# Plain float32 second products for the whole first tile, doubled zeros' products in the front, and two steps of the weight conversion moved from VectorE to GpSimd

## The chip, the cores and the metric

The kernel runs on one core of one Trainium2 chip. The metric is the device time of one execution in microseconds (us), taken as the median of the runs shown. TensorE is called PE in the profile, VectorE DVE, ScalarE ACT, GpSimd POOL and SyncE SP; PEld is the loading of weights into TensorE. SP issues the DMAs.

## The reference

A gated linear attention (an mLSTM) over 4 batches, 8 heads, 768 steps and head width 40 gives `x` of 3072 rows and 320 columns; behind it stands a feed-forward layer with a smooth rectifier.

```python
for t in range(S):
    m_new = np.maximum(f_gate[:, :, t] + m, i_gate[:, :, t])
    f_stab = np.exp(f_gate[:, :, t] + m - m_new); i_stab = np.exp(i_gate[:, :, t] - m_new)
    C = f_stab * C + i_stab * einsum('bhd,bhe->bhde', vt, kt)
    n = f_stab * n + i_stab * kt
    y[:, :, t] = sigmoid(o_gate) * einsum('bhde,bhe->bhd', C, qt) / np.maximum(abs(n . qt), 1.0)
x = y.transpose(0, 2, 1, 3).reshape(3072, 320)
h = x @ w_in                                                 # 320 -> 2048
g = np.where(h >= 1, h, np.where(h <= -1, 0, (h + 1) ** 2 / 4))
out = g @ w_out                                              # 2048 -> 320
```

## The kernel before

The 768 steps are cut into 6 chunks of 128 (L), so there are 24 blocks `n` = chunk x 4 + batch. Four blocks make one tile `j` of 512 rows for the feed-forward layer, so there are 6 tiles. `w_in` is worked through in 16 slices `fc` of 128 columns. `mm1(j, fc)` is 8 matmuls of 128x512 into a PSUM tile `psh`, of which there are two, and three passes (`r`: a relu and a square on ACT, a maximum and minimum on DVE) make `g` of it. `mm2` multiplies `g` by the same slice of `w_out` (128 rows of 320 columns) into four PSUM tiles `pso`, one for each 128 rows of the tile, two steps `x` after its `mm1` (LAG = 2).

Float32 products are made in one of two ways. In the split way both operands are parted into a rounded high part and a rest (`gh`, `gl` from `r`; `oh` and `ol` from the weights) and three fp32r matmuls are made per 128 rows. In the plain way one float32 matmul is made of `r` and of the unparted weights `of`; the profile shows such a matmul as two records and its names as `pso<-ow,r`. `PLAIN_FC` says for how many slices of tile 0 the second products are plain. The weights of these slices are then parted in tile 1, at the even `fc`.

The weights come in as 64-bit words (the host passes float32 seen in another layout) and are converted on the chip by `words`: ACT makes the magnitude `mg`, one engine puts the sign into the upper 16-bit half of each word (`halves[:, :, 1]`), GpSimd the low bits into the lower half (`halves[:, :, 0]`), a maximum clamps `mg`, and a DVE instruction (`SCALAR_TENSOR_TENSOR win<-mg,win` or `ow<-mg,ow`) shifts and joins them. Pieces of `w_in` have 128x768 elements (`win`, from `wraw`), pieces of `w_out` 128x640 (`ow`). There are 8 of each; one piece of `w_in` is converted in the front, the others during tile 0 by `split_next`, which runs ahead of `fc` by `DUE`. After `words`, `split` makes the rounded part `wh` on ACT and the rest `wl` on DVE; the first products need both. `win` and `mg` have one buffer each, so a conversion waits for the one before it.

Ahead of tile 0 stands the front: the attention of the blocks 0 to 3, written out by hand as the list `STEPS`. `E` and `A` are the products that make a block's matrix of exponents in PSUM, `x` its exponentials on ACT, `s` the scores on PE, `m` their product on DVE, `h` the transposition of the gates, `v` a scaling of `v` on GpSimd, `u` the matmuls with `v`, `y`, `z` and `t` the rest of a block. `w1` means: one matmul of zeros (128x512, bf16) ahead of the next product that opens a PSUM tile; its result is overwritten. `w9` at the start makes nine.

During tile 0 the attention of the blocks 4 and on runs in slots `slot(FRONT + x)`. Its parts: `select` (GpSimd, `AFFINE_SELECT Abc`) masks the sums that a DMA from `a_d` has spread over all rows, `decay` (ACT, 8 activations `Abc<-Abc,nA`), `score`, `main` and `carry_on` (`C`). The gates of a chunk (`gate_piece`) are some 17 small DVE instructions of 32 rows, from the scan `m<-fi_t` to `ex<-m,ah`.

Within `STEPS` the program order of each engine is as written. Behind it the framework's scheduler sets the order of each engine's instructions, so an edit in one place can move the instructions of others. Every engine works through its own list strictly in that order.

Of the kernel before, what the change touches and what calls it, by code (L numbers as in the profile page):

```python
# [13 lines left out]
ALU = mybir.AluOpType  # L14
# [17 lines left out]

LAG = 2

PLAIN_FC = 4

# [13 lines left out]


STEPS = (
# [3 lines left out]
)  # L58

HALF = 64  # L60
# [4 lines left out]
TINY = 2.0  # L65
# [30 lines left out]
def mlstm_ffn_kernel(ctx, tc, qk, qn, vk, og, fi0, fi, w_in, w_out, cst, out):  # L96
    nc = Core(tc)
# [197 lines left out]
    def words(out, raw):  # L295

        n = raw.shape[1] * raw.shape[2] // 2
        hi = raw.rearrange("p k (f w) -> p (k f) w", w=2)[:, :, 1]  # L300
        quarter = raw.rearrange("p k f -> p (k f)").bitcast(U16).rearrange("p (f w) -> p f w", w=4)
        out = out.rearrange("p k f -> p (k f)").bitcast(I32)
        halves = out.bitcast(U16).rearrange("p (f w) -> p f w", w=2)
        mg = stage.tile([P, n], F32, name="mg", bufs=1)
        nc.scalar.activation(mg, hi.bitcast(F32), AF.Abs, scale=65536.0)
        nc.vector.tensor_scalar(out=halves[:, :, 1], in0=quarter[:, :, 3], scalar1=0x8000, scalar2=None,
                                op0=ALU.bitwise_and)

        nc.gpsimd.tensor_scalar(out=halves[:, :, 0], in0=quarter[:, :, 1], scalar1=1 / 8192, scalar2=-4095.5 / 8192,
                                op0=ALU.mult, op1=ALU.add)  # L310
        nc.vector.tensor_scalar_max(mg, mg, TINY)
        nc.vector.scalar_tensor_tensor(out=out, in0=mg.bitcast(I32), scalar=3, in1=out,
                                       op0=ALU.logical_shift_left, op1=ALU.bitwise_or)

# [18 lines left out]
    def convert(kind, i):  # L333
        raw = raws.pop((kind, i))
        if kind == "in":
            sl = slice(2 * i * P, 2 * (i + 1) * P)
            w = stage.tile([P, 3, 2 * P], F32, name="win", bufs=1)
            words(w, raw)
            yield
            yield from split(wh[:, :, sl], wl[:, :, sl], w)  # L340
        else:
            of[i] = ow.tile([P, 656], F32, name="ow")[:, :2 * DM].rearrange("p (k e) -> p k e", k=2)
            words(of[i], raw)
            if 2 * i >= PLAIN_FC:
                yield
                yield from split_out(i)
# [283 lines left out]
    for n in range(NS):  # L630
        j, r = divmod(n, NTC)
        s0 = FRONT + OFFS[n - B] if j else 0
# [10 lines left out]
    def slot(i):  # L643
        for n, kind in sorted(plan.get(i, ()), key=lambda x: (list(order).index(x[1]), x[0])):
            if (n, kind) not in gens:
                gens[n, kind] = order[kind](n)
            next(gens[n, kind])
            c, b = divmod(n, B)
            if kind == "main":
                at[n] = at.get(n, 0) + 1  # L650
                if b == 0 and at[n] == 1:
                    with behind(("r", "act")):
                        sigmoid(c)
                if b == B - 1 and at[n] == 1 and c + 1 < NC:
                    load_og(c + 1)
# [18 lines left out]
    def parts(r):  # L674
        gh = mo.tile([P, TT], F32R, name="gh", bufs=3)
        nc.scalar.copy(gh, r)
        gl = mo.tile([P, TT], F32R, name="gl", bufs=3)
        nc.vector.tensor_tensor(out=gl, in0=r, in1=gh.bitcast(F32), op=ALU.subtract)
        return gh, gl
# [110 lines left out]
    for x in range(NG + LAG):  # L790
        j, fc = divmod(x, NFC)
        if x < NG:
# [6 lines left out]
            if fc == 0:  # L799
                ops[j] = [ps_o.tile([P, 512], F32, name="pso") for _ in range(NTC)]  # L800
            if j == 1 and fc % 2 == 0 and fc < PLAIN_FC:
                with tc.issue_after(mark["r", "act"].ins), tc.issue_after(mark["r", "dve"].ins):
# [11 lines left out]
            with behind(("v", "pool")):  # L814
                slot(FRONT + x)
            gs[x] = parts(r) if j or fc >= PLAIN_FC else (r,)
        if x >= LAG:
# [60 lines left out]
```

## Time and profile before

| | |
|---|---|
| median of 3 runs | 534.55 us (534.29 to 538.14) |
| profiled execution: its own time, its span | 537.02 us, 535.2 us |
| PE, DVE, ACT, POOL busy | 501.2, 370.9, 297.0, 147.3 us |
| granted TensorE clock, mean | 0.945 of full speed |
| first product of tile 0 | at 36.6 us |
| first product of tile 1 | at 151.85 us |

The span is 1.8 us shorter than the profiled execution's own time. A row of the timeline gives the start in us, the duration in us, the engine, the source line, the operation, what it writes and reads and how many instructions are merged; in brackets stands the idle time before it and what ended that. A row of a window gives its length, each engine's busy time with the number of its instructions, the granted clock and the DMAs' share.

### The profile page before, as it was taken

How to read it: one execution, taken by the hardware profiler on the slowest of the kernel's cores; microseconds unless marked ns; L12 is line 12 of the kernel's file. 1: busy time of each engine (PE TensorE's matmuls, PEld its weight loads, DVE VectorE, ACT ScalarE, POOL GpSimd, SP SyncE). 2: the span in 40 equal slices, each digit the busy share in tenths (PEclk: the TensorE clock that was granted, in tenths of full speed). 3: DMA queues.
4: the chain of work that ended last, by engine and by line, in shares of the span. 5: the costliest groups of instructions: out<-in, count | busy, mean ns of one | idle time of the engine just before them, and what ended most of it. 6: DMA issues, size and time to landing. Idle time of an engine off the chain costs nothing.

```text
span 535.2 us, 9288 instructions
## 1 busy us (share of the span) xinstructions
PE 501.2 (94%) x3563; PEld 432.8 (81%) x3563; DVE 370.9 (69%) x689; ACT 297.0 (55%) x588; POOL 147.3 (28%) x148
## 2 busy tenths in 40 slices
PE   8985979998999999989999979899999999999996
PEld 5763768777879889978888858688888898989985
DVE  5579989888879767768576849777657766443342
ACT  6235777644748563467644435755468344455553
POOL 4115513333433223433052515143411212000000
PEclk9577989967999999999999979899999999999999
DMA  8837454454252213251122234032333100010001
GB/s 245 261 114 241 157 182 151 139 185 153 80 156 72 57 51 103 79 171 58 29 79 69 87 103 149 3 91 91 112 105 114 39 1 1 1 50 1 0 1 50
DMA packets 29648, 51.31 MB, mean 96 GB/s; under 512 B 10124, under 2 KB 20004, under 8 KB 29604
## 3 DMA queue, kind: packets, MB, share of 16 engines
q1 hardware_dynamic: 29604, 50.72, 30.3%
q8 instruction: 28, 0.46, 0.4%
q14 instruction: 16, 0.13, 0.1%
HBM read 46.67 MB, written 4.04 MB: 95 GB/s over the span
## 4 chain that ended last, share of the span: by engine, by line
PE 59%; DVE 8%; ACT 7%; DMA 2%; issue 1%; POOL 1%; ACTq 0%; POOLq 0%
PE psh L79 26%; PE pso L79 21%; PE psa L79 11%; ACT Abc L79 2%; ACT r L79 2%; DMA Abc<-a_d 2%; DVE r L79 1%; DVE z L79 1%; ACT L79 1%; DVE gl L79 1%; DMA out<-r 1%; DVE ow L79 1%; ACT gh L79 1%; DVE C L79 1%; POOL Abc L79 1%
## 5 line engine op out<-in xcount | busy, mean ns | idle before, releaser
L79 ACT ACTIVATE r<-psh,half 128x512 f32<-128x512 f32 x96 | 65.3, 684 | 101.9 <-PE psh L79 98.8
L79 PE MATMUL psh<-xh,wh 128*128 128x512 f32 x288 | 106.1, 426 | 13.3 <-DVE r L79 10.9
L79 PE MATMUL pso<-ow,gh 128*128 128x320 f32 x368 | 113.9, 312 | 1.0 <-DVE ow L79 1.0
L79 PE MATMUL pso<-oh,gh 128*128 128x320 f32 x368 | 112.8, 315 | 0.0
L79 DVE SCALAR_TENSOR_TENSOR r<-psh,r 128x512 f32<-128x512 f32 x96 | 65.8, 686 | 65.7 <-ACT r L79 65.3
L79 PE MATMUL pso<-oh,gl 128*128 128x320 f32 x368 | 105.2, 311 | 0.0
L79 PE MATMUL psh<-xh,wl 128*128 128x512 f32 x288 | 102.3, 411 | 0.1
L79 DVE TENSOR_TENSOR gl<-r,gh 128x512 fp32r<-128x512 f32 x92 | 67.2, 733 | 30.4 <-ACT gh L79 29.4
L79 ACT CAST gh<-r 128x512 fp32r<-128x512 f32 x92 | 56.7, 617 | 51.7 <-DVE r L79 50.8
L79 PEld LDWEIGHTS pso<-ow,gh 128*128 128x128 f32 x368 | 69.6, 189 | 4.2 <-DVE ow L79 1.2
L79 PEld LDWEIGHTS pso<-oh,gh 128*128 128x128 f32 x368 | 69.0, 189 | 4.4 <-ACT gh L79 0.2
L79 PEld LDWEIGHTS psh<-xh,wh 128*128 128x128 f32 x288 | 52.9, 200 | 24.1 <-DVE r L79 12.5
L79 PEld LDWEIGHTS psh<-xh,wl 128*128 128x128 f32 x288 | 56.4, 198 | 14.0 <-DVE wl L79 0.8
L79 PEld LDWEIGHTS pso<-oh,gl 128*128 128x128 f32 x368 | 66.7, 188 | 0.6
L79 PE MATMUL psh<-xl,wh 128*128 128x512 f32 x192 | 62.7, 408 | 0.0
L79 ACT ACTIVATE r<-r 128x512 f32<-128x512 f32 x96 | 60.2, 632 | 2.2
L79 ACT ACTIVATE Abc<-Abc,nA 128x128 f32<-128x128 f32 x160 | 49.5, 389 | 19.0 <-POOL Abc L79 18.8
L79 POOL TENSOR_TENSOR m<-m 128x1024 bf16<-128x1024 f32 x16 | 32.0, 1999 | 56.3 <-DVE m L79 45.3
L79 POOL TENSOR_TENSOR v<-vk,G 128x328 f32<-128x328 f32 x36 | 31.0, 864 | 54.4 <-issue 31.6
L79 PEld LDWEIGHTS psh<-xl,wh 128*128 128x128 f32 x192 | 37.6, 197 | 8.9
L79 POOL TENSOR_TENSOR C<-C,dec 120x369 f32<-120x369 f32 x16 | 14.6, 910 | 89.2 <-PE psa L79 89.2
L79 PE MATMUL psa<-raw 40*128 40x128 f32 x320 | 33.9, 300 | 3.5 <-ACT nA L79 1.7
(187 smaller groups left out, 709.3 us busy)
## 6 DMA issues: line engine op xcount, KB each, us to landing
Abc<-a_d SPq DMA_DIRECT2D x20, 512.0 KB
raw<-in_qk SPq DMA_DIRECT2D x48, 160.0 KB
vk<-in_vk SPq DMA_DIRECT2D x20, 324.0 KB
wraw<-in_w_in SPq DMA_DIRECT2D x8, 768.0 KB
wraw<-in_w_out SPq DMA_DIRECT2D x8, 640.0 KB
sig<-in_og SPq DMA_DIRECT2D x6, 640.0 KB
out<-r SPq DMA_DIRECT2D x24, 160.0 KB
qn<-in_qn SPq DMA_DIRECT2D x20, 180.0 KB
```

What stands on the lines that cost most here:

```text
L79: r = getattr(self.engine, name)(*args, **kwargs)
```

## The change

`PLAIN_FC` goes from 4 to 16: all second products of tile 0 are plain. The weights of `w_out` are no longer parted in tile 0, and all 8 pieces are parted in tile 1, where 2 were before; the parting of `r` into `gh` and `gl` falls away in tile 0 for 12 of 16 slices. In `STEPS` each `w1` but one becomes `w2`, and `E1 A1` with a `w1` of its own moves from ahead of `k0` to behind `m00`. In `words` the sign becomes a comparison and a multiplication on GpSimd, and the clamp of `mg` moves there too.

```diff
-PLAIN_FC = 4
+PLAIN_FC = 16
...
-    "Lg Li Lo Lq0 Lv0 Lq1 Lw0 Lf Lq2 Lv2 Lq3 Lw1 Lc o w9 E0 g0 p A0 E1 A1 k0 x00 w1 s0 h0 x01 m00 v0 x10 m01 w1 s1 "
-    "x11 v1 m10 c w1 u0 m11 w1 E2 A2 x20 w1 s2 y0 x21 v2 m20 m21 w1 u1 z0 w1 E3 A3 x30 e w1 s3 v3 y1 x31 t0 m30 m31 "
-    "w1 u2 z1 y2 w1 u3 t1 z2 y3 w1 t2 z3 t3 d g1 "
+    "Lg Li Lo Lq0 Lv0 Lq1 Lw0 Lf Lq2 Lv2 Lq3 Lw1 Lc o w9 E0 g0 p A0 k0 x00 w2 s0 x01 m00 w1 E1 A1 h0 v0 x10 m01 w2 s1 "
+    "x11 v1 m10 c w2 u0 m11 w2 E2 A2 x20 w2 s2 y0 x21 v2 m20 m21 w2 u1 z0 w2 E3 A3 x30 e w2 s3 v3 y1 x31 t0 m30 m31 "
+    "w2 u2 z1 y2 w2 u3 t1 z2 y3 w2 t2 z3 t3 d g1 "
...
-        nc.vector.tensor_scalar(out=halves[:, :, 1], in0=quarter[:, :, 3], scalar1=0x8000, scalar2=None,
-                                op0=ALU.bitwise_and)
+        nc.gpsimd.tensor_scalar(out=halves[:, :, 1], in0=quarter[:, :, 3], scalar1=32768.0, scalar2=32768.0,
+                                op0=ALU.is_ge, op1=ALU.mult)
...
-        nc.vector.tensor_scalar_max(mg, mg, TINY)
+        nc.gpsimd.tensor_scalar(out=mg, in0=mg, scalar1=TINY, scalar2=None, op0=ALU.max)
```

The order of the instructions moves with it. On PE in the front, ahead of the scores of block 0 and behind the sums of block 0 (`pick` are the sums' selecting columns, `raw` the scores, `late_t,idb` the mask that opens a block's exponents), what is added is marked with +:

```order
 L82 LDWEIGHTS pick
 L82 MATMUL psh<-ac_179,pick 128x128
+L82 LDWEIGHTS zeros
+L82 MATMUL pso<-zeros 128x512
+L82 LDWEIGHTS zeros
+L82 MATMUL pso<-zeros 128x512
+L82 MATMUL pso<-raw 128x128 x8
+L82 LDWEIGHTS zeros
+L82 MATMUL pso<-zeros 128x512
 L82 LDWEIGHTS idb
 L82 MATMUL pso<-late_t,idb 128x512
```

The scores of block 0 with two zeros' products now stand ahead of block 1's exponents, where they stood behind them with one.

On ACT in the first slices of tile 0, from the conversion's `wh` of the second piece of `w_in`, before:

```order
L79 ACTIVATE r<-psh,half 128x512
L79 ACTIVATE r<-r 128x512
L79 CAST wh<-win 128x3x256
L79 ACTIVATE mg<-wraw 128x640
L79 ACTIVATE r<-psh,half 128x512
L79 ACTIVATE r<-r 128x512
L79 ACTIVATE G<-psa 128x128
L79 ACTIVATE nA<-psa 128x32
L79 ACTIVATE Abc<-Abc,nA 128x128 x12
L79 ACTIVATE mg<-wraw 128x768
```

And there in the changed kernel (the first `r<-psh` here is that of the third slice):

```order
L79 CAST wh<-win 128x3x256
L79 ACTIVATE mg<-wraw 128x640
L79 ACTIVATE G<-psa 128x128
L79 ACTIVATE nA<-psa 128x32
L79 ACTIVATE Abc<-Abc,nA 128x128 x16
L79 ACTIVATE r<-psh,half 128x512
L79 ACTIVATE mg<-wraw 128x768
L79 ACTIVATE Abc<-Abc,nA 128x128 x4
L79 ACTIVATE r<-psh,half 128x512
L79 ACTIVATE Abc<-Abc,nA 128x128 x4
L79 ACTIVATE r<-r 128x512 x2
```

The 24 exponentials of the blocks 4 to 6 now stand ahead of the squares `r<-r` of the third and fourth slice, and these ahead of the next `wh`; before, the squares and that `wh` came first. On DVE the two `r<-psh,r` of these slices stand ahead of the gates of chunk 2 in the changed kernel, and the join of the third piece (`win<-mg,win`) behind all but two of the gates' instructions. On SP the three DMAs that spread the sums of chunk 1 (`Abc<-a_d`) stood behind the load of the third piece of `w_in` and stand ahead of it.

On POOL at the same place, from the conversion of the second piece of `w_in` on, before:

```order
L79 TENSOR_SCALAR win<-wraw 128x768
L79 TENSOR_TENSOR ow<-ow,G 128x328 x2
L79 TENSOR_SCALAR win<-wraw 128x768
L79 TENSOR_SCALAR ow<-wraw 128x640
L79 COPY ex<-fi_t 32x128
L79 TENSOR_TENSOR ow<-ow,G 128x328
L79 AFFINE_SELECT Abc<-Abc 128x1024 x3
L79 TENSOR_TENSOR v_630<-vk,G 128x328
L79 TENSOR_TENSOR v_770<-vk,G 128x328
```

And in the changed kernel, from the clamp of that piece on:

```order
L79 TENSOR_SCALAR mg<-mg 128x768
L79 TENSOR_SCALAR win<-wraw 128x768 x2
L79 COPY ex<-fi_t 32x128
L79 AFFINE_SELECT Abc<-Abc 128x1024 x2
L79 TENSOR_SCALAR mg<-mg 128x640
L79 AFFINE_SELECT Abc<-Abc 128x1024
L79 TENSOR_TENSOR v_642<-vk,G 128x328
L79 TENSOR_TENSOR v_779<-vk,G 128x328
L79 TENSOR_SCALAR win<-wraw 128x768 x2
L79 TENSOR_SCALAR ow<-wraw 128x640 x2
L79 TENSOR_TENSOR ow<-ow,G 128x328
L79 TENSOR_SCALAR mg<-mg 128x768
```

Each piece now has three passes on POOL. Those of the third piece of `w_in` (the second `win<-wraw`) stood ahead of the three selects and now stand behind them and behind both scalings of `v`.

## The prediction

> **What bounds the kernel now.** I read the page's busy times first, then windows of the span, then the timeline at the places where PE waits.
>
> ```profile
> span 535.2 us, 9288 instructions
> PE 501.2 (94%) x3563; PEld 432.8 (81%) x3563; DVE 370.9 (69%) x689; ACT 297.0 (55%) x588; POOL 147.3 (28%) x148
> ...
> 12.37:26.02 13.65, 13.65 (x73) 11.09 (x72) 7.97 (x17) 3.82 (x13) 2.49 (x3) 0.50 0.90 264
> ...
> 36.60:157.50 120.90, 106.69 (x606) 88.82 (x606) 104.97 (x184) 74.14 (x151) 47.60 (x44) 0.87 0.51 163
> ...
> 36.60:59.25 22.65, 16.70 (x56) 12.19 (x56) 22.38 (x44) 10.86 (x19) 12.16 (x10) 0.78 0.84 281
> 59.25:157.50 98.25, 89.99 (x554) 76.63 (x552) 82.60 (x141) 63.28 (x133) 35.43 (x34) 0.90 0.43 136
> 157.50:300.00 142.50, 139.52 (x1096) 123.54 (x1093) 106.11 (x198) 84.09 (x171) 47.45 (x43) 1.00 0.27 81
> ```
>
> In a window's row stand its length, the busy time of PE, PEld, DVE, ACT and POOL, and the granted clock. PE is the bound over the whole, but not everywhere. From 157.5 to 300 us it works at full clock and idles 2% (139.52 of 142.50). In tile 0, from 36.6 to 157.5 us (157.5 is where the products of block 8 with `v` end, with 18 first and 16 second products done), it is DVE that is full: 104.97 of 120.90 us, in the first 22.65 us even 22.38. PE idles there 14.2 us and has a clock of 0.87. In the front, from 12.37 to 26.02 us, PE is busy without a gap and yet at half clock. The change touches these two places; what lies behind 157.5 us it touches only through the parting of weights in tile 1.
>
> **The change part by part. Plain second products cost PE time.** A plain slice and a split slice, each up to what follows it, at full clock:
>
> ```profile
> 65.84 2.32 PE L79 MATMUL pso<-ow,r 128*128 128x320 f32 x8
> 67.99 0.27 PE L79 MATMUL psa<-ident,ex 128*128 128x128 f32 x1
> ...
> 463.31 0.31 PE L79 MATMUL pso<-oh,gh 128*128 128x320 f32 x1
> ...
> 465.04 0.63 PE L79 MATMUL psh<-xh,wh 128*128 128x512 f32 x2
> ```
>
> The plain slice takes 67.99 - 65.84 = 2.15 us, the split one 465.04 - 463.31 = 1.73. Twelve slices more are plain: 12 x 0.42 = 5.0 us of PE.
>
> **What leaves DVE in tile 0**, by groups of 36.6 to 157.5 us:
>
> ```profile
> L79 DVE TENSOR_TENSOR gl<-r,gh 128x512 fp32r<-128x512 f32 x12 | 8.8, 742 | 1.1 <-ACT gh L79 1.1
> ...
> L79 DVE TENSOR_TENSOR ow<-ow,oh 128x640 fp32r<-128x640 f32 x7 | 7.0, 1006 | 0.0
> ...
> L79 DVE TENSOR_SCALAR win<-wraw 128x768 uint16<-128x768 uint16 x7 | 6.1, 875 | 0.1
> L79 DVE TENSOR_SCALAR ow<-wraw 128x640 uint16<-128x640 uint16 x8 | 4.8, 602 | 0.7 <-DMA wraw<-in_w_out 0.6
> L79 DVE TENSOR_SCALAR mg<-mg 128x768 f32<-128x768 f32 x7 | 4.7, 677 | 0.0
> L79 DVE TENSOR_SCALAR mg<-mg 128x640 f32<-128x640 f32 x8 | 4.6, 578 | 0.0
> ```
>
> The 12 `gl` go (8.8), six of the seven `ol` move to tile 1 (6 x 1.0 = 6.0), and the sign and the clamp go to POOL (6.1 + 4.8 + 4.7 + 4.6 = 20.2). DVE keeps 105 - 35 = 70 us. That ends DVE as the bound of tile 0.
>
> **What comes to POOL.** The sign is of the kind that POOL does already for the low bits; the clamp, one float32 input on POOL at this size, is not in the trace.
>
> ```profile
> L79 POOL TENSOR_SCALAR win<-wraw 128x768 uint16<-128x768 uint16 x7 | 10.4, 1482 | 24.5 <-DVE wl L79 13.3 <-issue 7.9 <-DVE ac L82 2.0
> ...
> L79 POOL TENSOR_SCALAR_AFFINE_SELECT Abc<-Abc 128x1024 f32<-128x1024 f32 x7 | 8.8, 1257 | 8.2 <-DMA Abc<-a_d 8.2
> L79 POOL TENSOR_SCALAR ow<-wraw 128x640 uint16<-128x640 uint16 x7 | 7.2, 1027 | 10.0 <-DMA wraw<-in_w_out 7.1 <-PE psh L79 2.8
> ```
>
> Signs: 7 x 1.48 + 8 x 1.03 = 18.6 us. For the clamp the bounds are the select's time by elements (1257 x 768/1024 = 0.94 us and 0.79) and that of the low bits (1.48 and 1.03); I take the lower, the select being float32 too: 7 x 0.94 + 8 x 0.79 = 12.9, at most 18.6. POOL goes from 47.6 to 79 us, at most 85, of some 115: it fits, but it is no longer idle, and everything queued behind a pass waits.
>
> **Term 1, the front.** How zeros' products and the narrow products go at half and full clock:
>
> ```profile
> 19.95 3.48 PE L82 MATMUL psa<-ow,Abc 128*128 128x41 f32 x16
> ...
> 23.23 0.88 PE L82 MATMUL psa<-ident,y 128*128 128x128 f32 x3
> 23.90 0.63 PE L82 MATMUL psh<-zeros 128*128 128x512 bf16 x1
> 24.32 1.06 PE L82 MATMUL psh<-late_t,idb 128*128 128x512 bf16 x2
> ...
> 26.03 0.38 PE L82 MATMUL pso<-zeros 128*128 128x512 bf16 x1
> ...
> 27.66 1.87 PE L82 MATMUL pso<-ow,Abc 128*128 128x41 f32 x16
> 29.37 0.52 PE L82 MATMUL pso<-ident,y 128*128 128x128 f32 x3
> ```
>
> The same 16 narrow matmuls take 3.28 us at half clock (19.95 to 23.23) and 1.71 at full. A zeros' product takes 0.42 us at half (23.90 to 24.32), so 0.21 at full; the exponents of a block take 1.71 (24.32 to 26.03), so 0.86. What brings the clock up at 26.02 is a window that ends with wide, full-height products (zeros, `late_t`, `pick`); what stood ahead, narrow products of 41 columns or of 40 rows, kept PE busy and did not. In the changed program the window ahead of the drop at 12.37 us holds block 1's exponents (0.86 us, from before that window) and three more zeros' products (0.63) of 3.41 us; I expect that the clock then stays up. Halving the 13.65 us gives 6.8; the change has 12 zeros' products more, 12 x 0.21 = 2.5: **-4 us**. If the clock doesn't stay up, four of them lie in the half-clock stretch and eight outside: 4 x 0.42 + 8 x 0.21 = +3.4. PE sets the end of the front, since ACT and DVE have 3.82 and 7.97 of those 13.65 us. The moved `E1 A1` costs at most its 0.86 us ahead of `h0`, hidden behind the exponentials on ACT; without that cover it is lost.
>
> **Term 2, from tile 0's first product to that of slice 4** (36.6 to 59.25 us). Here the order speaks against the change.
>
> ```profile
> 2.83 0.48 DVE L82 TENSOR_TENSOR_SCAN m<-fi,m 96x128 f32<-96x128 f32 x1 [1.90 <-DMA fi<-in_fi]
> ...
> 6.43 0.14 DVE L82 COPY carry<-m 32x1 f32<-32x1 f32 x1
> ...
> 47.95 1.22 PE L79 MATMUL psh<-xh,wh 128*128 128x512 f32 x2 [5.95 <-DVE r L79]
> ...
> 52.53 2.37 POOL L79 TENSOR_SCALAR_AFFINE_SELECT Abc<-Abc 128x1024 f32<-128x1024 f32 x2 [1.18 <-DMA Abc<-a_d]
> ...
> 59.66 3.31 ACT L79 ACTIVATE Abc<-Abc,nA 128x128 f32<-128x128 f32 x11
> ...
> L79 ACT ACTIVATE r<-psh,half 128x512 f32<-128x512 f32 x18 | 12.0, 678 | 9.6 <-PE psh L79 9.5
> L79 ACT ACTIVATE r<-r 128x512 f32<-128x512 f32 x18 | 11.1, 629 | 0.3
> ...
> L79 ACT CAST wh<-win 128x768 fp32r<-128x768 f32 x7 | 5.8, 825 | 12.6 <-DVE win L79 12.6
> ...
> L79 DVE SCALAR_TENSOR_TENSOR r<-psh,r 128x512 f32<-128x512 f32 x16 | 10.8, 681 | 3.6 <-ACT r L79 3.4
> ...
> L79 DVE SCALAR_TENSOR_TENSOR ow<-mg,ow 128x640 int32<-128x640 int32 x8 | 7.5, 933 | 0.0
> ...
> L79 DVE SCALAR_TENSOR_TENSOR win<-mg,win 128x768 int32<-128x768 int32 x7 | 6.6, 948 | 0.2
> ```
>
> Slice 2 waited 5.95 us, to 47.95. DVE loses the passes ahead of it, but POOL now does three passes where it did one; I leave that start as it is (a gain of 2 us and a loss of 2 are both possible). Then ACT has 24 exponentials ahead of the squares of slices 2 and 3. They can begin when the selects have the spread sums: 52.5 before, some 2 us earlier now, since SP issues these DMAs ahead of a weight load; with a select of 1.2, at about 51.5. ACT: 24 x 0.30 + 2 x 0.68 + 2 x 0.63 = 9.8, to 61.3. DVE must then finish `r` of both and all of chunk 2's gates, since the join stands behind them: the same recurrences of chunk 0 took 3.7 us (2.83 to 6.57), two `r` and the join take 2 x 0.68 + 0.95 = 2.3, and `wh` on ACT is 0.83: 68.1 for slice 4 instead of 59.25, **+9**. In that time two carries and more are done that came later before (1.3 us): **+8**. Bounds: +3, if ACT starts on the second exponentials late anyway and DVE's gates fall into the gap; +11, if the DMAs land as before.
>
> **Term 3, from slice 4 to the mark at 157.5.** Before: 98.25 us, PE busy 89.99, clock 0.90. A clock of 0.90 is a fifth of the time at half; half of that is lost, 0.10 x 98.25 = 9.8. So PE's work at full clock is 80.2 us, and with the plain products 85.2, less the 1.3 done already, 83.9. With DVE relieved (about 58% where it was 84%), I take the idle share of the stretch behind 157.5 us, 2%, so 1.8, and one half-clock window after the wait of term 2, 1.7: 87.4, **-11**. Bounds: -14 (no idle at all), and 0 (below, the shared port).
>
> **Term 4, tile 1.** Six more partings of weights, 6 x 1.0 us on DVE and as many casts on ACT, lie beside PE in a stretch where DVE has 106 of 142.5 us. I take **+1**; if that cover were gone, 6.
>
> Sum: -4 + 8 - 11 + 1 = -6 us against the profiled execution's span of 535.2, which lies 1.8 us under its own time of 537.02 and is within 0.1% of the median of 534.55. I set the -6 against the median: **528.5 us**.
>
> **The rivals.**
>
> *The clock stays low in the front.* For it: PE was busy in all of 12.37 to 26.02 us and the clock was 0.50 all the same, so busy time alone does not lift it. Against it: the lift at 26.02 came with wide products. Price: +3.4 instead of -4, so 535.9. The Trainium skill, in "TensorE: Matmul & The Clock Gate", section "What's actually happening", says that one busy window of some 3.4 us releases the clock and an idle one throttles it; by PE's busy time that is contradicted by this stretch, and by it zeros' products could not help where PE never idles.
>
> *POOL and DVE share a port, and POOL becomes the bound (the slower side).*
>
> ```profile
> 38.45 2.22 POOL L79 TENSOR_SCALAR win<-wraw 128x768 uint16<-128x768 uint16 x1 [7.87 <-issue]
> ...
> 39.65 1.24 DVE L82 TENSOR_TENSOR_SCAN m<-fi_t,m 32x128 f32<-32x128 f32 x1
> ```
>
> A scan that takes 0.48 us alone (2.83) took 1.24 beside a POOL pass, and that pass 2.22 where the mean is 1.48: each waited for the other. If POOL's passes and DVE's conversion steps go one after the other, a pair of slices needs 2 x 1.48 + 0.94 and 2 x 1.03 + 0.79 on POOL, two joins and `wl` on DVE (0.95 + 0.93, and 0.95 for `wl`, which I take like the join), ACT's 0.83, and POOL's attention, (47.6 - 10.4 - 7.2) / 8 = 3.8: 14.2 us. From slice 4 there are 7 pairs to the mark: 99 us. Above 12.5 us for a pair (87.4 / 7) POOL decides; at 14.2 term 3 is +1 instead of -11, and the sum is +6: 540.5. Against it: POOL's own sum is at most 85 of 115 us. The Trainium skill, in "SBUF — State Buffer", section "SBUF: two separate sides", calls the port pair of DVE and GpSimd an exclusive lock that is held for a whole instruction. The two rows above agree; by this rule moving passes from DVE to GpSimd relieves the port of nothing.
>
> *The early wait of term 2 does not come, and the rest does.* ACT gets its sums early and slice 4 starts as before: -4 + 0 - 13 + 1 = -16, so 518.5.
>
> *DVE was full but not the limit*, since PE waited for chains of attention that remain: term 3 is -3, the sum +2 with the front's gain: 536.5.
>
> **How the numbers follow.** My forecast, 524 to 533, has 0.45; the missing early wait (517 to 523) 0.13; the low clock 0.18; DVE not the limit 0.12; the shared port 0.12. The predicted time is that of the forecast. A measurement tells about 1% (5.3 us, so 529.2 and 539.9) from no change. Of the forecast about 0.30 lies below 529.2, with the 0.13 that is 0.43 for faster; for slower I count 0.10 of the port and 0.07 of the two cases near 536, 0.17; 0.40 remain. The range goes from 518 to 540.5: it leaves out a little at each end, no more than 2 in 10.
>
> **What would show it.** The clock in 12.37 to 26.02 us at 1.00 and tile 0's first product near 32.6 us (term 1); PE idle for 6 to 9 us ahead of slice 4, behind a DVE join or `wh` (term 2); PE at 95% or more behind that, DVE under 65% (term 3); no gap above 0.5 us in tile 1 (term 4). POOL passes of `win` above 1.6 us in the mean, or PE waiting for DVE joins that wait for POOL's clamps throughout tile 0, would make it wrong on the slow side; an early start of slice 4 on the fast side.

## The result and the profile after

The changed kernel takes 550.99 us in the median of 4 runs (549.08 to 551.92), the kernel before 534.42 in the 4 beside them (530.65 to 538.14). The ratio is **1.0292, 95% interval 1.0230 to 1.0353**: slower by 2.9%, where 528.5 us was forecast and the range ended at 540.5. The ratios here leave out disturbed runs; the medians are over all runs.

The page of the changed kernel: busy times, and the chain that ended last by engine (that of before has POOL with 1%).

```profile
span 548.9 us, 9190 instructions
PE 504.5 (92%) x3527; PEld 427.5 (78%) x3527; DVE 352.2 (64%) x645; ACT 291.7 (53%) x576; POOL 232.5 (42%) x180
...
PE 64%; POOL 17%; DVE 7%; issue 5%; ACT 4%; DMA 2%; ACTq 0%; POOLq 0%; DVEq 0%
```

DVE is relieved (370.9 to 352.2 us) and POOL has gone from 147.3 to 232.5, 85 us more over the whole span, where the forecast gave it 31 to 37 more in tile 0. And POOL is on the chain.

Windows by the prediction's terms, before (first four rows) and after (the others): from tile 0's first product to that of slice 4, from there to that of slice 18, from there to that of tile 2, and the rest. The columns are as before.

```profile
36.61:59.25 22.64, 16.69 (x56) 12.18 (x56) 22.36 (x44) 10.85 (x19) 12.16 (x10) 0.78 0.84 281
59.25:159.26 100.01, 91.16 (x569) 77.60 (x567) 84.24 (x146) 65.02 (x134) 36.17 (x35) 0.90 0.43 138
159.26:231.06 71.80, 70.85 (x558) 63.19 (x558) 56.15 (x104) 42.54 (x90) 23.83 (x23) 1.00 0.27 82
231.06:535.20 304.14, 289.85 (x2184) 256.36 (x2184) 187.22 (x340) 162.63 (x305) 67.12 (x60) 0.98 0.19 60
...
36.69:69.81 33.12, 20.50 (x68) 15.50 (x69) 22.67 (x46) 18.76 (x48) 29.10 (x19) 0.71 0.46 156
69.81:174.47 104.66, 93.43 (x449) 72.09 (x449) 60.23 (x93) 49.14 (x88) 92.16 (x53) 0.85 0.39 132
174.47:248.79 74.32, 73.35 (x617) 65.14 (x615) 60.65 (x111) 45.26 (x94) 25.65 (x24) 1.00 0.29 88
248.79:548.90 300.11, 288.25 (x2184) 255.16 (x2184) 188.87 (x340) 162.59 (x305) 67.75 (x60) 0.99 0.20 60
```

| stretch | before | after | difference | forecast |
|---|---|---|---|---|
| front | 36.61 | 36.69 | +0.1 | -4 |
| first product to slice 4 | 22.64 | 33.12 | +10.5 | +8 |
| slice 4 to slice 18 | 100.01 | 104.66 | +4.7 | -11 |
| rest of tile 1 | 71.80 | 74.32 | +2.5 | +1 |
| behind tile 1 | 304.14 | 300.11 | -4.0 | 0 |
| span | 535.2 | 548.9 | +13.7 | -6 |

(The last row but one is PE's idle time, 14.3 against 11.9 us, and the clock; the change touches nothing there.) These are windows of one execution each. The kernel before, profiled once more below, had 21.75 us in the second row and 104.97 in the third. So the 10.5 us ahead of slice 4 are clear of what two executions of one kernel differ by, and the 4.7 behind it are not.

In tile 0 POOL is busy 29.10 + 92.16 = 121.3 us of 137.8, DVE in the second stretch 60.23 of 104.66: the bound went from DVE to POOL. POOL's work alone is nearly as long as both stretches together were before (122.65). The chain that ended last shows it too; between slice 4 and slice 18 its shares by line are (the view ends the row there):

```profile
by line: POOL win L79 18.9%; POOL mg L79 17.6%; issue 16.4%; POOL ow L79 13.9%; PE psh L79 10.8%; PE pso L79 8.1%; POOL v L79 4.7%; POOL Abc L79 3.3%; POOL C L79 3.1%; DVE win L79 2.3%; PE psa L79 1.0%; DVE xl L79 0.3%; DVE xh L79 0.3%; POO
```

The passes of the conversion on POOL are half of it (18.9 + 17.6 + 13.9%). POOL's groups from 36.69 to 174.47 us, busy time and mean of one:

```profile
L79 POOL TENSOR_SCALAR win<-wraw 128x768 uint16<-128x768 uint16 x14 | 31.9, 2278 | 1.0
L79 POOL TENSOR_SCALAR ow<-wraw 128x640 uint16<-128x640 uint16 x14 | 25.5, 1819 | 1.0
L79 POOL TENSOR_SCALAR mg<-mg 128x640 f32<-128x640 f32 x8 | 17.2, 2150 | 6.8 <-ACT mg L79 6.7
L79 POOL TENSOR_SCALAR mg<-mg 128x768 f32<-128x768 f32 x7 | 15.8, 2252 | 3.3 <-ACT mg L79 2.9
```

Signs and low bits together take 57.4 us, where the forecast had 18.6 + 10.4 + 7.2 = 36.2; the clamps take 33.0, where it had 12.9. A pair of slices costs POOL 2 x 2.28 + 2.25 + 2 x 1.82 + 2.15 = 12.6 us of conversion, and with the forecast's 3.8 of attention 16.4.

The front: its window, POOL's first conversion (shortest, median and longest of a sign and a low-bit pass), then who waits for its clamp:

```profile
12.37:26.02 13.65, 10.26 (x80) 7.72 (x79) 6.64 (x15) 3.83 (x14) 8.70 (x6) 0.87 0.88 265
...
L82 POOL TENSOR_SCALAR win<-wraw x2: 1062/2062/3062, 12.7 to 15.8; 128x768 uint16<-128x768 uint16 x2
...
16.96 2.14 POOL L82 TENSOR_SCALAR mg<-mg 128x768 f32<-128x768 f32 x1
19.13 1.48 DVE L82 SCALAR_TENSOR_TENSOR win<-mg,win 128x768 int32<-128x768 int32 x1 [6.24 <-POOL mg L82]
...
21.27 1.09 PE L82 MATMUL psa<-ow,Abc 128*128 128x41 f32 x8 [2.83 <-DVE Abc L82]
```

DVE stood idle for 6.24 us here, and yet the sign took 3.06 us and the clamp 2.14: they are long by themselves, not through DVE. The join waits for the clamp, the product `m` (`Abc<-psh,Abc`) stands behind the join on DVE, and PE waits for that, 2.83 us.

### The profile page after: what moved, and what is told of

The parts are those of the page before. It is cut to its first block, busy times and chain, and to the rows that moved or that the text cites. A ratio compares the mean times of both kernels' runs of the same rounds, so it can differ in the third digit from the quotient of the medians.

```text
span 548.9 us, 9190 instructions
## 1 busy us (share of the span) xinstructions
PE 504.5 (92%) x3527; PEld 427.5 (78%) x3527; DVE 352.2 (64%) x645; ACT 291.7 (53%) x576; POOL 232.5 (42%) x180
## 4 chain that ended last, share of the span: by engine, by line
PE 64%; POOL 17%; DVE 7%; issue 5%; ACT 4%; DMA 2%; ACTq 0%; POOLq 0%; DVEq 0%
PE psh L79 28%; PE pso L79 25%; PE psa L79 10%; POOL win L79 4%; POOL mg L79 4%; POOL ow L79 4%; DMA Abc<-a_d 2%; POOL v L79 1%; POOL Abc L79 1%; ACT r L79 1%; ACT Abc L79 1%; POOL win L82 1%; DVE gl L79 1%; DVE z L79 1%; POOL C L79 1%
## 5 line engine op out<-in xcount | busy, mean ns | idle before, releaser
L79 PE MATMUL pso<-oh,gh 128*128 128x320 f32 x320 | 99.3, 313 | 0.0
L79 PE MATMUL pso<-ow,gh 128*128 128x320 f32 x320 | 98.4, 310 | 0.0
L79 PE MATMUL pso<-oh,gl 128*128 128x320 f32 x320 | 92.7, 312 | 0.0
L79 DVE TENSOR_TENSOR gl<-r,gh 128x512 fp32r<-128x512 f32 x80 | 62.3, 779 | 29.4 <-ACT gh L79 28.1
L79 ACT CAST gh<-r 128x512 fp32r<-128x512 f32 x80 | 49.5, 619 | 51.8 <-DVE r L79 49.5
L79 PEld LDWEIGHTS psh<-xh,wh 128*128 128x128 f32 x288 | 55.2, 207 | 18.1 <-ACT wh L79 4.3
L79 PEld LDWEIGHTS pso<-oh,gh 128*128 128x128 f32 x320 | 60.1, 188 | 3.5
L79 PEld LDWEIGHTS pso<-ow,gh 128*128 128x128 f32 x320 | 60.2, 188 | 2.8
L79 PEld LDWEIGHTS pso<-oh,gl 128*128 128x128 f32 x320 | 58.2, 188 | 0.8
L79 ACT ACTIVATE Abc<-Abc,nA 128x128 f32<-128x128 f32 x160 | 49.3, 389 | 17.8 <-POOL Abc L79 17.6
L79 POOL TENSOR_SCALAR mg<-mg 128x640 f32<-128x640 f32 (+1 forms) x15 | 33.0, 2198 | 10.0 <-ACT mg L79 9.6
```

Source lines behind the costliest of these rows:

```text
L79: r = getattr(self.engine, name)(*args, **kwargs)
```

## The experiments

"Price theory": a sign or a clamp costs POOL far more than I charged, and POOL's sum is the limit of tile 0. Against it stand the port theory (the passes are long because DVE holds a shared port), the wait theory (the loss is the scheduler's order ahead of slice 4) and the chain theory (the round of magnitude, clamp and join through one buffer). First the parts of the change, apart. Rows are windows from slice 4 to slice 18 unless said otherwise.

**Both conversion steps back on DVE**

```diff
-        nc.gpsimd.tensor_scalar(out=halves[:, :, 1], ... op0=ALU.is_ge, op1=ALU.mult)
+        nc.vector.tensor_scalar(out=halves[:, :, 1], ... op0=ALU.bitwise_and)
-        nc.gpsimd.tensor_scalar(out=mg, in0=mg, scalar1=TINY, scalar2=None, op0=ALU.max)
+        nc.vector.tensor_scalar_max(mg, mg, TINY)
```

> The changed kernel with the sign and the clamp back on DVE; the plain second products and the front's new list stay. Price theory (the two moved passes cost POOL far more than the 1.48 and 0.94 us charged: 3.06 and 2.14 us in the front of the changed kernel, where DVE stood idle, and POOL is then the limit of tile 0): the loss goes, slice 4 starts at 59 to 62 us, POOL is under 50 us in tile 0, the median is 525 to 532 us. Wait theory (the loss comes from the order, ACT's 24 exponentials ahead of the squares before slice 4, whoever converts): slice 4 still starts behind 66 us and the median is 536 to 543. In the front the join of the first piece no longer waits for POOL's clamp, so the gap of 2.83 us at 18.44 goes and the first product of tile 0 comes at 32.5 to 34 us instead of 36.7.

Measured: 533.14 us, ratio 0.9948 (0.9891 to 1.0005), one us above the price theory's range. First product to slice 4, then slice 4 to slice 18, in a profiled execution of 537.54 us, 4 us above the median:

```profile
32.04:54.55 22.51, 16.56 (x55) 12.22 (x56) 22.27 (x40) 10.72 (x19) 11.65 (x11) 0.73 0.78 281
54.55:158.32 103.77, 94.94 (x520) 73.63 (x518) 73.72 (x132) 55.04 (x116) 35.50 (x35) 0.90 0.42 133
```

The loss is gone, and the wait ahead of slice 4 with it (22.51 us). But on ACT the squares of slices 2 and 3 stand ahead of the exponentials again in this kernel, so that it doesn't part the wait theory from the price theory; the last experiment does. The front reaches tile 0 at 32.04 us. The second stretch, 103.77 us, is no shorter than before (100.01 and 104.97 in two profiles); the next experiment but one bears on that.

**The conversion alone** (the kernel before, with the two lines of the change)

> The kernel before with only the sign and the clamp on POOL. Price theory: POOL needs about 3.1 + 1.06 + 2.2 + 2.6 + 0.92 + 2.2 = 12.1 us for a pair of slices plus some 3.8 of attention, 16 us where the pair took 12 to 14 before: 14 to 20 us slower, 548 to 555. Wait theory: the order of ACT decides; if the 24 exponentials do not stand ahead of the squares here, the time is within 4 us of before. DVE theory (DVE's full list was the limit of tile 0 and relief from 20 us of passes pays): 522 to 530.

Measured: 561.34 us, ratio 1.0493 (1.0408 to 1.0578), even above the expected 548 to 555. From slice 4:

```profile
73.34:182.20 108.86, 92.16 (x498) 77.33 (x498) 71.97 (x110) 58.38 (x104) 90.36 (x53) 0.84 0.38 127
```

POOL has 90 us here as in the changed kernel. The conversion is the whole loss; without the other parts it is larger. Tile 0's first product came at 40.57 us, 4 us later than in the changed kernel.

**The plain products alone** (`PLAIN_FC = 16` in the kernel before)

> The kernel before with only PLAIN_FC = 16. It costs PE 12 x 0.42 = 5.0 us and takes 8.8 (the rests of r) and 6.0 us (six partings) from DVE in tile 0, which was full there: if DVE is the limit of tile 0, the gain is 8 to 10 us on DVE less nothing on PE, 525 to 529; if chains of attention are the limit and DVE only full, it is the 5 us of PE, 537 to 540. I expect 530.

Measured: 536.57 us, ratio 1.0031 (0.9973 to 1.0088). From slice 4, and the front:

```profile
54.95:159.25 104.30, 94.88 (x520) 73.50 (x518) 76.66 (x131) 55.30 (x116) 35.87 (x35) 0.90 0.42 134
...
12.37:26.02 13.65, 13.45 (x115) 10.83 (x114) 9.06 (x20) 7.45 (x24) 3.15 (x3) 0.87 0.89 258
```

In the stretch from slice 4 the kernel before, profiled once more, had:

```profile
58.48:163.45 104.97, 94.19 (x568) 80.05 (x566) 87.56 (x151) 65.21 (x134) 36.95 (x36) 0.87 0.43 134
```

DVE falls from 84.24 and 87.56 us to 76.66, and the stretch lies between the two of the kernel before. PE idles 9.4 us, where it idled 8.9 and 10.8: the relief of DVE did not take away its waits. My own figure of 530 was missed. The interval leaves -1.4 to +4.7 us, and 5.0 is what the plain products were to cost PE, so what the relief bought in time is not resolved.

**The front's list alone**

> The kernel before with only the new list of the front. If the clock stays up from 12.37 us as it did in the changed kernel (at 1.00 up to 22.4 us), the first product of tile 0 comes 3 to 4 us earlier, at about 33 us, and the median is 529 to 532. If tile 0 is bound by the conversion on DVE from the start, not by the first product, half of it is lost there: 532 to 535. Low clock: 537 to 538.

Measured: 533.63 us, ratio 0.9979 (0.9935 to 1.0023). The front's stretch:

```profile
12.37:26.02 13.65, 13.28 (x122) 10.68 (x124) 10.18 (x22) 7.52 (x24) 2.79 (x4) 1.00 0.90 266
```

The clock stays at 1.00, and the first product comes at 31.13 us. In the time it isn't resolved: the interval reaches over 1.

**The kernel before once more**, for its front

> The kernel before once more, for a second look at its front. If the half clock from 12.37 to 26.02 us belongs to the old list of the front, it shows again and the first product of tile 0 comes at 36.6 us. If it belongs to where the clock's windows of 3.41 us happen to lie in that execution, the front is shorter or the half-clock stretch lies elsewhere, as in the kernel with only the plain products, which has the old list and reached tile 0 at 32.64 us.

```profile
12.37:26.02 13.65, 13.65 (x77) 10.94 (x77) 8.29 (x17) 3.97 (x14) 3.14 (x3) 0.56 0.90 259
```

The half clock lasts as long here as in the first profile, with PE busy in all of it; it only begins 1.5 us later:

```profile
13.88:27.53 13.65, 13.65 (x75) 10.57 (x76) 7.09 (x16) 4.14 (x14) 2.69 (x3) 0.50 0.88 258
```

In the three profiles of the old list with the conversion on DVE the clock from 12.37 to 26.02 us was 0.50, 0.56 and (plain products alone) 0.87, and the first product came at 36.61, 36.73 and 32.64 us. So two of three executions of the old list have the long stretch at half clock and one has not; the profile that I took the term from was one of the two, and none of the three had 1.00. With the new list and the clamp on DVE the clock was 1.00 there and tile 0 began at 31.13 to 32.81 us in all four profiles that computed the sign.

**The sign on POOL by a multiplication and an addition** (with zero, so the signs are left out)

```diff
-        nc.gpsimd.tensor_scalar(out=halves[:, :, 1], ... scalar1=32768.0, scalar2=32768.0, op0=ALU.is_ge, op1=ALU.mult)
+        nc.gpsimd.tensor_scalar(out=halves[:, :, 1], ... scalar1=0.0, scalar2=0.0, op0=ALU.mult, op1=ALU.add)
```

> The changed kernel, where the sign pass on POOL is a multiplication and an addition with zero (the same reads and writes; the signs of the weights are left out). Price theory: the operation makes the length, so the pass takes 1.06 and 0.91 us like the low bits instead of 3.06 and 2.57; a pair of slices on POOL falls from 16.3 to about 12.6 us, no more than PE and DVE need, and the median is 533 to 541. Port theory (POOL's passes are long because DVE holds the port): the pass stays at 2 us and more, 547 to 551.

Measured: 538.46 us, ratio 1.0035 (0.9992 to 1.0078), as the price theory expected. POOL's group of signs and low bits, from 36 us:

```profile
L79 POOL TENSOR_SCALAR win<-wraw 128x768 uint16<-128x768 uint16 x14 | 16.7, 1196 | 3.6 <-DVE wl L79 3.1
```

The same number of passes, in the same place of the program, on the same data; the mean over signs and low bits is 1.20 us instead of 2.28. The operation makes the length, and the length the loss. PE still waited 6.52 us ahead of slice 4 in this kernel, and what is left of the loss is within noise.

**Only the sign on POOL**, and **only the clamp on POOL** (the changed kernel, the other back on DVE)

> The changed kernel with the clamp back on DVE, the sign on POOL. Price theory: POOL's pair falls by the two clamps, 2.2 + 2.1 us, from 16.3 to 12; that is at the edge: 534 to 542, about half of the loss gone. Chain theory (it is the clamp between ACT's magnitude and the join, not POOL's sum, that makes tile 0 late): 528 to 534, as with both on DVE.

> The changed kernel with the sign back on DVE, the clamp on POOL. Price theory: POOL's pair falls by the two signs, 3.1 + 2.6 us and what DVE adds to them, from 16.3 to about 10.4: POOL is no longer the limit, 530 to 537. Chain theory: the clamp stays in the chain with its 2.2 us, 543 to 550.

Measured: 536.07 us, ratio 1.0023 (0.9981 to 1.0065), and 531.95 us, ratio **0.9919 (0.9891 to 0.9948)**; both within the price theory's ranges and outside the chain theory's, the first by 2 us, the second by 11.

```profile
60.08:158.25 98.17, 91.53 (x511) 71.97 (x511) 62.47 (x108) 48.63 (x91) 66.56 (x43) 0.92 0.45 147
...
56.75:154.93 98.18, 88.98 (x517) 67.99 (x517) 74.14 (x120) 56.92 (x120) 61.69 (x47) 0.97 0.46 147
```

POOL is at 68% and 63% of the stretch, and both stretches are shorter than before. The costs of the two steps don't add up: against the kernel with both on DVE the medians say +2.9 (sign), -1.2 (clamp) and +17.9 us (both). A limit that is reached only with both behaves so. The clamp on POOL, beside the other two parts of the change, is the one version computing the signs that is clear of noise faster than the kernel before, by 0.8%; that it is faster than with both steps on DVE is not resolved.

**Neither step on any engine** (low bits written as whole words; the signs are left out)

> The changed kernel without sign and clamp on any engine (the low bits are written as whole words; signs of weights are left out). It tells what relief of DVE by these 20 us is worth when it costs no engine anything. If DVE is the limit of tile 0 (the forecast's term 3): 8 to 11 us faster than with both on DVE, 521 to 526. If PE waits for the chains of attention and for the clock, not for DVE: within 3 us of the kernel with both on DVE, 530 to 534.

Measured: 526.29 us, ratio 0.9820 (0.9754 to 0.9887).

```profile
51.24:148.73 97.49, 90.28 (x520) 70.37 (x518) 60.23 (x106) 54.41 (x116) 31.52 (x35) 0.95 0.45 141
```

This is an upper estimate of what the move could have brought: 7 us against the kernel with both on DVE, between what the two theories gave. (It is generous: the low-bit passes are shorter here too, 0.90 us for `win` and for `ow`.) DVE is busy 60.23 us here as in the changed kernel (60.23), so DVE's work is not what makes 97.49 us there into 104.66; that POOL's passes make all of it isn't shown, since the kernel before alone varied by 5 us in this stretch.

**What a POOL pass costs by its operation.** A program of POOL passes of 128x768 alone; names begin with `u` (uint16) or `f` (float32), and then give the operations.

> A program that only times POOL passes of 128x768, four of each form, first with DVE idle and then beside a row of DVE subtractions of 128x768; nothing of the kernel's work is done. If a comparison or a maximum is dear on POOL whatever the type: is_ge and max at 2 to 3 us, multiplication and addition at 1.05, in uint16 and float32 alike, and is_ge with a multiplication 3.06. If it is the float32 type that is dear: every float32 pass at 2.1. Beside DVE, price theory: each form grows by under 0.7 us; port theory: the passes of both engines go one after the other and each form grows by 1 us or more.

```profile
L115 POOL TENSOR_SCALAR u_ge<-raw 128x768 uint16<-128x768 uint16 x4 | 9.5, 2372 | 0.0
...
L122 POOL TENSOR_SCALAR f_mul<-src 128x768 f32<-128x768 f32 x4 | 8.5, 2132 | 0.0
...
L115 POOL TENSOR_SCALAR u_mul_add<-raw 128x768 uint16<-128x768 uint16 x4 | 4.2, 1046 | 0.3
...
L122 POOL TENSOR_SCALAR f_mul_add<-src 128x768 f32<-128x768 f32 x4 | 3.3, 832 | 0.3
```

I had put it to comparison against arithmetic; that is wrong. A single multiplication (2.13 us) costs 2.6 times a multiplication with an addition (0.83; below, the short form). All POOL passes but the last two had ended before DVE began, so this program says next to nothing on the port. The second program does, and tries more pairs:

> Again only POOL passes of 128x768, four of each, in program order, with DVE idle, and behind them three forms beside a row of DVE subtractions (in the first such program they had ended before DVE began). Of the first program: multiplication with addition took 0.83 us in float32 and 1.05 in uint16, every single operation 2.13 and 2.37, maximum with addition 2.78, comparison with multiplication 3.03. If only the pair multiplication and addition has a short form, the other pairs take 2.8 us; if every pair of arithmetic operations has one, addition with multiplication and twice multiplication take 0.83 too, and those with a maximum 2.8. Beside DVE: price theory, each form grows by under 0.7 us; port theory, by 1 us or more.

Four POOL groups; then the passes beside DVE (`b`), and DVE's subtractions beside the comparison, the short form and the maximum, and alone:

```profile
L82 POOL TENSOR_SCALAR f_add_add<-src 128x768 f32<-128x768 f32 x4 | 11.1, 2781 | 0.2
L82 POOL TENSOR_SCALAR f_mul_max<-src 128x768 f32<-128x768 f32 x4 | 11.1, 2775 | 0.2
...
L82 POOL TENSOR_SCALAR f_add_mul<-src 128x768 f32<-128x768 f32 x4 | 3.3, 833 | 0.2
L82 POOL TENSOR_SCALAR f_mul_mul<-src 128x768 f32<-128x768 f32 x4 | 3.3, 832 | 0.2
...
L82 POOL TENSOR_SCALAR b_ge_mul<-raw 128x768 uint16<-128x768 uint16 x4 | 13.3, 3327 | 0.2
L82 POOL TENSOR_SCALAR b_mul_add<-raw 128x768 uint16<-128x768 uint16 x4 | 6.2, 1548 | 0.3
...
L82 DVE TENSOR_TENSOR da<-f_mul_max,src 128x768 f32<-128x768 f32 x6 | 6.8, 1137 | 0.2
L82 DVE TENSOR_TENSOR da<-f_mul_max,src 128x768 f32<-128x768 f32 x5 | 7.4, 1488 | 0.2
L82 DVE TENSOR_TENSOR da<-f_mul_max,src 128x768 f32<-128x768 f32 x9 | 11.3, 1255 | 0.3
L82 DVE TENSOR_TENSOR da<-f_mul_max,src 128x768 f32<-128x768 f32 x7 | 6.7, 958 | 0.2
```

Beside DVE the passes grow by 0.3 (comparison, 3.03 to 3.33) and 0.5 us (short form, 1.05 to 1.55), and a subtraction from 0.96 to 1.14 and 1.49 us. In one comparison pass DVE ends 3.33 / 1.14 = 2.9 subtractions: the engines don't take turns by whole instructions, so the port theory's size is wrong. Its sign is right: the short form slows DVE by half.

**The sign on POOL as two passes of the short form** (the clamp back on DVE)

```diff
+        nc.gpsimd.tensor_scalar(out=halves[:, :, 1], in0=quarter[:, :, 3], scalar1=1 / 32768, scalar2=-16383.5 / 32768,
+                                op0=ALU.mult, op1=ALU.add)
+        nc.gpsimd.tensor_scalar(out=halves[:, :, 1], in0=halves[:, :, 1], scalar1=32768.0, scalar2=0.0,
+                                op0=ALU.mult, op1=ALU.add)
```

> The changed kernel with the clamp back on DVE and the sign on POOL as two passes of the short form, each a multiplication and an addition (first q/32768 rounded to 0 or 1, then times 32768): 2 x 1.05 and 2 x 0.91 us instead of 3.03 and 2.57. POOL's pair is 3 x 1.05 + 3 x 0.91 + 3.8 = 9.7 us and DVE has the sign's 0.87 + 0.60 less. Price theory: POOL is not the limit, and since the clamp is not in the chain behind ACT, 527 to 532, 0.8 to 1.5% faster than before. If any third pass on POOL brings back the wait ahead of slice 4 (as the sign alone did, 27.8 us from the first product instead of 22.5): 534 to 538.

Measured: 539.43 us, ratio 1.0076 (1.0034 to 1.0118): a miss: no better than with the one dear sign pass (536.07), though the first product to slice 4 took only 21.74 us. The second stretch, then the sums over both stretches, here and in the kernel with only the sign on POOL:

```profile
54.55:160.87 106.32, 96.45 (x519) 74.45 (x517) 74.41 (x123) 54.72 (x117) 64.52 (x61) 0.90 0.44 138
...
sum 128.06, PE 113.56 PEld 86.23 DVE 95.31 ACT 65.18 POOL 80.91; mean PE 56.78 PEld 43.12 DVE 47.66 ACT 32.59 POOL 40.45
...
sum 126.00, PE 109.36 PEld 85.19 DVE 86.55 ACT 66.06 POOL 88.35; mean PE 54.68 PEld 42.60 DVE 43.27 ACT 33.03 POOL 44.18
```

POOL is at 61% and no limit. DVE has the same work in both kernels and needs 95.31 us here instead of 86.55, as much as with both steps on it (95.99): what was taken off DVE came back as slower passes beside POOL's short ones, as in the second program. That this is all of the difference isn't shown.

**Two buffers for magnitude and joined piece** in the changed kernel (`bufs=1` to `bufs=2` for `mg` and `win`)

> The changed kernel with two buffers each for the magnitude and for the joined piece, so that a conversion no longer waits for the one before it. Throughput theory (POOL needs 16 us for a pair of slices whatever the order, and was busy 92.2 of 104.7 us from slice 4 on): only POOL's idle eighth can go, 546 to 551. Chain theory (ACT's magnitude, POOL's clamp and DVE's join take turns over one buffer, and that round is what lasts 16 us): 530 to 541.

Measured: 554.78 us, ratio 1.0389 (1.0268 to 1.0510), above the ranges of both theories. First product to slice 4, then two pieces of what follows, and POOL's largest wait in the second (in total, times, longest):

```profile
36.94:57.51 20.57, 15.31 (x48) 10.97 (x49) 16.47 (x34) 10.81 (x18) 18.60 (x8) 0.83 0.74 253
...
57.51:104.80 47.29, 35.88 (x156) 26.18 (x154) 24.78 (x33) 26.43 (x55) 45.54 (x29) 0.86 0.32 99
104.80:175.09 70.29, 63.71 (x371) 49.54 (x370) 42.82 (x76) 28.39 (x62) 45.91 (x35) 0.88 0.43 138
...
POOL C L79 <- PE psa L79: 10.0, 3, 5.7
```

The single buffer isn't it, so the chain theory falls. So does the wait theory: on ACT the squares stand ahead of the exponentials, the wait ahead of slice 4 is gone, 20.57 us instead of 33.12, and slice 18 comes at 175.09 us all the same (174.47). POOL is then full, 45.54 of 47.29 us. Behind 104.8 us it is busy 65% and stands in its list behind products of PE. POOL's sum in tile 0 is smaller here than in the changed kernel, 110.05 us against 121.26, and the time is not: the sum alone isn't the limit. How much of the loss POOL's order makes, and how much the sum, stays open.

## Why the prediction was wrong, step by step

**The failed step is the price of the passes on POOL** ("The sign is of the kind that POOL does already for the low bits"; the clamp by the select's time by elements). The bounds were rows of the same engine and type, one of them scaled to the shape, but of other operations. The sign takes 3.03 us where 1.48 was charged, the clamp 2.13 where 0.94 was. With these POOL's sum in tile 0 is 121 us, not 79 to 85, and "it fits" fails. The prediction's own sign of this came: passes of `win` on POOL took 2.28 us in the mean, where anything above 1.6 was to make it wrong on the slow side.

**Term 1, the front (-4, measured +0.1).** The clock did what was forecast: in the changed kernel it stayed up to 22.4 us, and alone the new list holds 1.00; that it is the wide products that count was not tested apart from the new order. With both steps back on DVE tile 0 began at 32.04 us, 4.6 earlier than before. What failed is again the move to POOL, which this term left out. The join of the first piece waits for POOL's clamp, and PE waited 2.83 us for that; with only the clamp on POOL tile 0 began at 34.06 us, with only the sign at 32.25, with both at 36.69. Besides, the gain has a base that varies: another execution of the old list reached tile 0 at 32.64 us. The Trainium skill's rule in "TensorE: Matmul & The Clock Gate", section "What's actually happening", under which a busy window releases the clock, is contradicted again: when the kernel before ran once more, PE was busy in all of 13.65 us at 0.50.

**Term 2, ahead of slice 4 (+8, measured +10.5).** Place and size are right, the size in part by luck: ACT ended the squares of slices 2 and 3 at 60.3 us (forecast 61.3), and DVE needed 6.9 us from there to the end of the join instead of 6.0. PE waited 8.76 us, up to the gates' `ex` behind that join.

```profile
59.18 1.14 ACT L79 ACTIVATE r<-r 128x512 f32<-128x512 f32 x2
59.83 0.69 DVE L79 SCALAR_TENSOR_TENSOR r<-psh,r 128x512 f32<-128x512 f32 x1 [3.84 <-ACT r L79]
...
66.32 0.94 DVE L79 SCALAR_TENSOR_TENSOR win<-mg,win 128x768 int32<-128x768 int32 x1
...
68.47 0.45 PE L79 MATMUL psa<-ident,ex 128*128 128x128 f32 x1 [8.76 <-DVE ex L79]
```

But it isn't a term of a sum: with two buffers it went, and the end of tile 0 stayed.

**Term 3, slice 4 on (-11, measured +4.7).** POOL as the limit was a rival, with 0.12 and 540.5 us; its direction was right, its price not. That DVE is full but not the limit, the rival with 536.5 us, fits the plain products alone, where DVE was relieved and PE idled as before; that they took 536.57 us is chance, since the rival's sum counts the front too. Nor is it the whole, as leaving both steps out brought 7 us. The assumption of 2% idle was wrong even without POOL's part: the plain products alone had 9% (9.42 of 104.30 us) and a clock of 0.90. What keeps the clock there isn't settled.

**Term 4 (+1, measured +2.5)**: the plain products alone, with six more partings in tile 1 as well, gave +1.2 there.

```profile
159.25:232.25 73.00, 71.30 (x559) 63.06 (x558) 60.37 (x110) 46.34 (x96) 24.30 (x23) 1.00 0.28 82
```

It is 73.00 us against 71.80. The other 1.3 us in the changed kernel weren't traced.

The rival's reading of the port ("each waited for the other") was too strong, and so is the rule cited there from the Trainium skill, "SBUF — State Buffer", section "SBUF: two separate sides" (an exclusive lock for a whole instruction): the second program's rows show both engines going on, each slower.

## What to carry to other kernels

Price an operation that moves to another engine by a row with the same operation there, not by one with the same shape and type; where there is none, time a row of such passes by themselves before the move. Relieving the fullest engine pays only as far as the next limit: leave the steps out altogether once, and the result (here 7 us) is an estimate of the most that any move can bring. A term that comes from one execution's clock needs a second execution, and so does a difference of a few us between two windows.

## What the runs showed of the hardware

A POOL pass of 128x768 with one input took 0.83 us in float32 when it was a multiplication with an addition, in either order, or two multiplications; a single multiplication, addition, maximum or comparison took 2.13, and two additions, a multiplication with a subtraction or a pair with a maximum 2.78. In uint16 it was 1.05, 2.37 and 3.03 (comparison with multiplication). DVE made the same float32 maximum in the kernel before in 0.54 us in the front and 0.68 in the mean of tile 0. The Trainium skill's page "GPSIMD Engine Reference", section "4.1 Engine selection", calls elementwise passes with one input on GpSimd roughly line-rate; beside DVE's 0.54 us only the short form, with 0.83, comes near that, and the maximum itself took 2.13.
